# Block-sparse attention and gated feed-forward on one core: keys and sampled copies in one tile, scores in fewer and wider matmuls

## The chip, the cores and the metric

One NeuronCore of one Trainium2 chip. The metric is the device time in microseconds of one execution of the whole program. A core has five engines that run their own instruction queues: TensorE (PE in the profile; its weight loads are listed apart as PEld), VectorE (DVE), ScalarE (ACT), GpSimd (POOL) and SyncE (SP, which here only issues DMAs).

## The reference

The inputs are q, k, v of 4 batches, 8 heads, 768 positions and 64 channels, and, for each of the 24 blocks of 32 positions, three sampled block numbers. Attention is masked by blocks, and its output goes through a two-layer feed-forward network:

```python
scores = scale * np.matmul(q, k.transpose(0, 1, 3, 2))
mask = np.abs(blk_i - blk_j) <= 1
mask = mask | (blk_i == 0) | (blk_j == 0) | (blk_i == n_blocks - 1) | (blk_j == n_blocks - 1)
...
        mask[qb * block:(qb + 1) * block, kb * block:(kb + 1) * block] = True
scores = np.where(mask, scores, -1000000000.0)
attn = softmax(scores)
x = (attn @ v) as [3072, 512]
h = x @ w_in
sp = np.maximum(h, 0.0) + np.log1p(np.exp(-np.abs(h)))
out = (h * erf(sp)) @ w_out
```

So a middle block of 32 queries attends to 8 blocks of keys, 256 columns: its own and its two neighbours (96 columns), its three samples (96), and the first and the last block of the sequence (64). The first and the last block of queries attend to all 768 positions.

## The kernel before, in words

The work is cut into units of scores, sixteen per batch. A unit "m" holds four query blocks (j = 0 to 3) of one group t and two pairs of heads (r = 0, 1) of a half called quad; its scores are a PSUM tile `s_m` of 128 partitions by 1024 columns. There are ten m units a batch. Units "e" (two a batch) hold the two query blocks that are left over; units "f" (four a batch) hold the first and the last query block, against all keys. Keys and queries are float32; a head pair fills the 128 rows of the contraction, and `qm` holds the queries so that one block of 32 queries of two heads is a stationary operand of 128 rows by 64 columns.

The keys of a batch stand in `kx` (one of two buffers), ordered by block by `order_k` (line 120). The sampled blocks are copied by GpSimd from `kx` into small tiles `kg` (line 330, `gather`; four of them, one per query block, three copies each). `key_columns` (line 554) gives for one query block the three operands that `scores` (line 565) multiplies: 96 columns of neighbours from `kx`, 96 of samples from `kg`, 64 of the two end blocks from `kx`. For an m unit `scores` runs over r, then over the three parts, then over the four query blocks:

```python
for r in range(2):
    for part in range(3):
        for j in range(4):
            o = slice((j % 2) * 64, (j % 2) * 64 + 64)
            c, e, keys = key_columns(b, 1 + 4 * t + j, slice(0, P), pr)[part]
            pe.matmul(s4[o, j // 2, r, c:e], q_, keys, start=True, stop=True)
```

That is 24 matmuls. Odd and even j write to the upper and the lower 64 partitions, and so use the two halves of the array's columns. Each float32 matmul is two passes in the trace, each with a weight load of its own, so a unit has 48 MATMUL and 48 LDWEIGHTS records.

Behind the scores come a row maximum on VectorE, exponentials on ScalarE, a split into two float16 parts, a transposing DMA, and, two units later (`PV_LAG`), the product with gathered values `vb` (PE writes `po`; `values`, line 605). The feed-forward network is woven in: every step of the main loop (from line 978) issues on PE, in this order, 24 matmuls of the first layer (`h`), the values of an older unit if there are any (`po`), the scores of the next unit if it is its turn, and 12 matmuls of the second layer (`o`). The order on every engine is that in which the program issues. The first m units are issued by hand ahead of the loop, while weights are being loaded and decoded. `spare_k` (line 432) is the second key buffer, lent to the weight decoding until the second batch's keys arrive.

Of the kernel before, what the change touches and what calls it, by code (L numbers as in the profile page):

```python
# [9 lines left out]
F32 = mybir.dt.float32  # L10
I32 = mybir.dt.int32
# [7 lines left out]
P = 128  # L19
BLOCK = 32  # L20
# [22 lines left out]
def sparse_attention_moe(ctx: ExitStack, tc: tile.TileContext, qT, kT, v, sampled, w_in, w_out, out):  # L43
# [22 lines left out]
    pe, act, dve, pool, sp = (InOrder(e) for e in (nc.tensor, nc.scalar, nc.vector, nc.gpsimd, nc.sync))  # L66
    B, H, D, S = qT.shape
    NB = S // BLOCK
# [4 lines left out]
    NR = sampled.shape[1]  # L73
    KT = S // P
    HP = H // 2
    VW = 2 * D + 2
    NM = NB - 2
    MT = 5
    KGS, VGS = 4, 8
# [8 lines left out]
    cp = ctx.enter_context(tc.tile_pool(name="cp", bufs=1))  # L88
    ld = ctx.enter_context(tc.tile_pool(name="ld", bufs=2))
    at = ctx.enter_context(tc.tile_pool(name="at", bufs=2))  # L90
# [8 lines left out]
    act.preload_act_table_set("natural_log_exp_and_others")  # L99


    kxs = {}
    samp2 = at.tile([P, NB, NR, 2], I32, tag="xf", name="samp2", bufs=1)
    samp = cp.tile([P, NB * NR], I32, tag="samp", name="samp")

# [12 lines left out]
        krs[b, pr] = kr  # L118

    def order_k(b, pr):  # L120
        if b not in kxs:
            kxs[b] = ld.tile([P, NB + 1, HP, BLOCK], F32, tag="kx", name=f"kx_{b}", bufs=2)
        kr = krs.pop((b, pr))
        copy = pool.tensor_copy if b else dve.tensor_copy if pr > 1 else act.copy
        copy(kxs[b][:, :NB, pr, :], kr.rearrange("p (n c) -> p n c", c=BLOCK))
        copy(kxs[b][:, NB, pr, :], kr[:, :BLOCK])

# [1 line left out]
    qm = cp.tile([P, HP, 4, 2, BLOCK], F32, tag="qm", name="qm")  # L131
# [183 lines left out]
    kgs = {}  # L315
    POOL, SYNC = mybir.EngineType.Pool, mybir.EngineType.SP

    def block_numbers(first, last, engine):

        (load,), blocks = nc.values_load_multi_w_load_instructions(  # L320
            samp[0:1, first * NR : last * NR],
            [engine],
            min_val=0,
            max_val=NB,
            skip_runtime_bounds_check_because="sampled blocks are numbers of the sequence's blocks",
        )
        tc.keep_in_program_order(load)
        return blocks

    def gather(b, t):  # L330

        first, last = 1 + 4 * t, min(5 + 4 * t, NB - 1)
        blocks = block_numbers(first, last, POOL)
        for i in range(first, last):
            kg = at.tile([P, NR, HP * BLOCK], F32, tag="kg", name=f"kg_{b}_{i}", bufs=KGS)
            for r in range(NR):
                n = blocks[(i - first) * NR + r]
                pool.tensor_copy(
                    kg[:, r : r + 1],
                    kxs[b].rearrange("p n a c -> p n (a c)")[:, bass.ds(n, 1), :],  # L340
                )
            kgs[b, i] = kg.rearrange("p r (a c) -> p r a c", c=BLOCK)

    PLACES = ((3, 0), (0, 1), (1, 1))
    ring = iter(range(B * (NM + 3)))
# [83 lines left out]
    def slots(t, at_slot, n):  # L429
        return t[:, at_slot : at_slot + n, :].rearrange("p n c -> p (n c)").bitcast(I32)  # L430

    spare_k = ld.tile([P, NB + 1, HP, BLOCK], F32, tag="kx", name="spare_k", bufs=2)
    spare_k = spare_k.rearrange("p n a c -> p (n a c)").bitcast(I32)
    wide = spare_k[:, 2048:3072]

    def raw_of(key, i, n):
# [9 lines left out]
    apart = {}  # L446
# [104 lines left out]
        transpose(pT, p2)  # L551
        pts[unit] = pT

    def key_columns(b, i, rows, pr):

        kx, kg = kxs[b], kgs[b, i]
        return (
            (0, 96, kx[rows, i - 1 : i + 2, pr, :]),
            (96, 192, kg[rows, :, pr, :]),
            (192, 256, kx[rows, 0 : NB : NB - 1, pr, :]),  # L560
        )

    pts = {}

    def scores(unit):
        kind, b, n = unit[0], unit[1], unit[2:]
        tag = "_".join(str(x) for x in unit)
        s = ps_s.tile([P, 1024], F32, tag="s", name=f"s_{tag}")
        if kind == "m":

            t, quad = n
            s4 = s.rearrange("p (h r w) -> p h r w", h=2, r=2)
            for r in range(2):
                pr = 2 * quad + r
                for part in range(3):
                    for j in range(4):
                        o = slice((j % 2) * 64, (j % 2) * 64 + 64)
                        q_ = qm[:, pr, j].rearrange("p a c -> p (a c)")
                        c, e, keys = key_columns(b, 1 + 4 * t + j, slice(0, P), pr)[part]
                        pe.matmul(s4[o, j // 2, r, c:e], q_, keys, start=True, stop=True)  # L580
            softs[unit] = (s, 4, 256)
        elif kind == "e":
            (quad,) = n
            s3 = s.rearrange("p (r w) -> p r w", r=HP)
            for r in range(2):
                for part in range(3):
                    for j in range(2):
                        o = slice(j * 64, j * 64 + 64)
                        q_ = qm[:, 2 * quad + r, j].rearrange("p a c -> p (a c)")
                        c, e, keys = key_columns(b, NB - 3 + j, slice(0, P), 2 * quad + r)[part]  # L590
                        pe.matmul(s3[o, r, c:e], q_, keys, start=True, stop=True)
            softs[unit] = (s[:, :512], 2, 256)
        else:
            (pr,) = n
            q_ = qm[:, pr, 2:].rearrange("p n a c -> p (n a c)")
            for c, e in ((0, 512), (512, S)):
                keys = kxs[b][:, c // BLOCK : e // BLOCK, pr, :]
                pe.matmul(s[:, c:e], q_, keys, start=True, stop=True)
            softs[unit] = (s[:, :S], 1, S)

    xTs = {}
# [184 lines left out]
    def gathers(m):  # L786

        nonlocal kfree, vfree
        if kjobs and kfree >= 4 and kjobs[0][0] in have_k:
            kfree -= 4  # L790
            gather(*kjobs.pop(0))
        room = 4 if begun > 0 else VGS
        while vjobs and vjobs[0][0] in have_v:
            b, i = vjobs[0]
            n = 2 if i > 0 else 1
            fresh = b > 0 and 0 < i < VGS
            if vfree < n or room < n * (1 + fresh):
                break
            vfree -= n
            room -= n * (1 + fresh)  # L800
            vjobs.pop(0)
            gather_v(b, i) if i > 0 else whole_v(b, -1 - i)
# [12 lines left out]
    def behind(m):  # L815

        b, n = divmod(m, per)
        if b + 1 < B:
            c = b + 1
            if n == 10:  # L820
                load_q(c, 0)
            k = n if b else 2 * (n - 10) if n > 9 else -1
            if k in ((1, 3, 5, 7) if b else (2, 4, 6, 8)):
                order_k(c, (k - 1) // 2)
            if k in (0, 2, 4, 6):
                load_k(c, k // 2)
            if k == 8:
                have_k.add(c)
            if b == 0:
                n -= 4  # L830
            if n in (1, 7):
                load_v(c, 0)
            if n == 3:
                load_v(c, 1)
            if n in (2, 4):
                square_v(c, n // 2 - 1)
            if n == 5:
                scale_v(c)
            if n in (5, 6):
                split_v(c, 1, n - 5)  # L840
            if n in (8, 9):
                split_v(c, 0, n - 8)
            if n == 9:
                have_v.add(c)
# [46 lines left out]
    for pr in range(HP):  # L891
        order_k(0, pr)
# [9 lines left out]
    for quad in range(2):  # L902
        square_v(0, quad)
    scale_v(0)
    scores(units[0])
    split_v(0, 0, 0)
    split_v(0, 0, 1)
# [7 lines left out]
    have_v.add(0)  # L915

    scores(units[1])
    used_keys(units[1])
    gathers(0)
# [9 lines left out]

    soft_turn(units[1])  # L930
    scores(units[2])
    work("Di4 Qi4 Di5")
    soft_max(units[2])
# [44 lines left out]
    for m in range(len(groups) + FF_LAG):  # L978
        ch, i = divmod(m, NGR)
        steps = 0  # L980
        if ch < len(until):
            first = until[ch - 1] if ch else FIRST
# [91 lines left out]
```

## Time and profile before

| | |
|---|---|
| median of 3 runs | 841.46 us (836.75, 841.46, 845.61) |
| span of the profiled execution | 836.8 us |
| PE busy | 710.8 us, 85% |
| ACT / DVE / POOL busy | 601.1 / 554.4 / 123.7 us |
| records on PE | 11100 MATMUL, 11100 LDWEIGHTS |

The lowest of the three runs is the span to the rounding, so the profiled execution's own time is taken as 836.8 us, with nothing lying around it; the median of the runs is 4.7 us above it. Busy time is a sum over records that overlap each other in the pipeline; how long a stretch of work takes PE is read from the starts of its records in the timeline.

### The profile page before, as it was taken

The numbers are of one execution on the slowest core, as the hardware profiler recorded it, in microseconds if no ns is written. First come the engines' busy times: TensorE is split into PE (matmuls) and PEld (weight loads), VectorE is DVE, ScalarE is ACT, GpSimd is POOL, SyncE is SP. The second block draws the span as 40 slices with busy tenths as digits, with TensorE's granted clock in tenths as the row PEclk, the third lists the DMA queues.
The fourth block names the chain that finished last, engine by engine and source line by source line (L and its number), as shares of the span: only waits on it lengthen the run. The fifth ranks groups of instructions, "written<-read, shape, count | busy, mean of one in ns | idle before, by whom it ended". The sixth has DMA issues, their size and how long they took to land.

```text
span 836.8 us, 26712 instructions
## 1 busy us (share of the span) xinstructions
PE 710.8 (85%) x11100; PEld 504.8 (60%) x11100; DVE 554.4 (66%) x977; ACT 601.1 (72%) x999; POOL 123.7 (15%) x344
## 2 busy tenths in 40 slices
PE   1253637899897899899999899999999899999997
PEld 1252424566665667566777666667777576766664
DVE  3994796887764766766566676756677567654454
ACT  4654657987865766887768778868678678776774
POOL 5430111001222220100201231000111100000000
PEclk9775867989998999999999999999999999999999
DMA  8999953687899697661497886633576758211000
GB/s 325 297 257 318 243 120 90 164 207 164 172 212 209 178 205 198 186 131 45 136 216 178 210 198 192 167 79 83 117 167 166 190 103 188 53 33 40 1 27 26
DMA packets 199930, 131.61 MB, mean 157 GB/s; under 512 B 144000, under 2 KB 167168, under 8 KB 199808
## 3 DMA queue, kind: packets, MB, share of 16 engines
q1 hardware_dynamic: 196384, 118.10, 58.1%
q0 software_dynamic: 3424, 11.80, 4.3%
q8 instruction: 87, 1.43, 0.7%
q14 instruction: 35, 0.29, 0.1%
HBM read 83.88 MB, written 12.95 MB: 116 GB/s over the span
## 4 chain that ended last, share of the span: by engine, by line
PE 47%; DVE 15%; issue 12%; ACT 10%; DMA 10%; SPq 2%; POOL 2%; POOLq 1%; ACTq 0%
PE h L59 18%; PE o L59 18%; PE s_m L59 5%; DMA vb<-vtab 4%; PE po L59 3%; DVE g L59 2%; ACT pf_m L59 2%; DVE q L59 2%; DVE mx_m L59 2%; DMA vtab<-vn 2%; SPq L59 2%; ACT x L59 2%; DVE p_m L59 2%; POOL kg L59 2%; ACT q L59 2%
## 5 line engine op out<-in xcount | busy, mean ns | idle before, releaser
L59 PE MATMUL h<-xT,wi 128*128 128x256 f16 x2304 | 274.2, 276 | 14.9 <-ACT wi L59 7.5
L59 PE MATMUL o<-wo,g 128*128 128x512 f16 x1152 | 270.3, 385 | 7.9 <-DVE wo L59 4.0
L59 PEld LDWEIGHTS <-wi 128*128 128x128 f16 x2304 | 227.4, 99 | 65.5 <-ACT wi L59 8.8
L59 PEld LDWEIGHTS <-g 128*128 128x128 f16 x1152 | 110.3, 99 | 133.0 <-issue 14.8
L59 ACT ACTIVATE x<-x 128x512 f32<-128x512 f32 x288 | 181.5, 630 | 9.1
L59 POOL COPY kg<-kx 128x128 f32 x264 | 90.5, 394 | 286.2 <-PE s_m L59 183.6
L59 ACT ACTIVATE pf_m<-s_m,nb_m 128x256 f32<-128x256 f32 x160 | 62.7, 475 | 65.4 <-DVE nb_m L59 59.5
L59 DVE SCALAR_TENSOR_TENSOR q<-x,q 128x512 f32<-128x512 f32 x96 | 66.7, 695 | 61.4 <-ACT x L59 60.1
L59 ACT ACTIVATE x<-h,isg 128x512 f32<-128x512 f32 x96 | 65.2, 680 | 36.3 <-PE h L59 35.7
L59 PE MATMUL s_m<-kx,qm 128*64 128x64 f32 (+1 forms) x1280 | 75.0, 249 | 6.8 <-ACT pf_m L59 4.2
L59 ACT ACTIVATE q<-q 128x512 f32<-128x512 f32 x96 | 59.5, 620 | 29.6 <-DVE q L59 29.6
L59 DVE SCALAR_TENSOR_TENSOR q<-q,h 128x512 f32<-128x512 f32 x96 | 65.5, 682 | 22.6 <-ACT q L59 22.6
L59 DVE TENSOR_TENSOR p_m<-pf_m,p_m 128x1024 f16<-128x1024 f32 x40 | 49.3, 1232 | 32.3 <-ACT p_m L59 32.3
L59 DVE SCALAR_TENSOR_TENSOR g<-q,g 128x512 f16<-128x512 f32 x96 | 67.0, 698 | 3.3
L59 PE MATMUL po<-vb,pT_m 128*32 128x65 f16 (+1 forms) x3840 | 44.7, 201 | 25.7 <-DMA vb<-vtab 15.0
L59 PEld LDWEIGHTS s_m<-kx,qm 128*64 128x64 f32 x1280 | 59.7, 146 | 10.4 <-ACT pf_m L59 4.9
L59 ACT ACTIVATE q<-x 128x512 f32<-128x512 f32 x96 | 60.5, 630 | 3.1
L59 DVE TENSOR_REDUCE mx_m<-s_m 128x4 f32<-128x1024 f32 x40 | 48.8, 1219 | 20.2 <-PE s_m L59 20.2
L59 PEld LDWEIGHTS <-pT_m 128*32 128x32 f16 x3840 | 38.0, 97 | 36.8 <-DMA vb<-vtab 16.3
L59 PE MATMUL s_m<-kg,qm 128*64 128x96 f32 x640 | 46.9, 261 | 3.2 <-POOL kg L59 2.2
L59 DVE TENSOR_TENSOR x<-xf,x 128x512 f16<-128x512 f32 x24 | 16.9, 703 | 43.3 <-ACT x L59 43.3
L59 DVE TENSOR_SCALAR g<-q 128x512 f16<-128x512 f32 x96 | 41.3, 431 | 3.3
(115 smaller groups left out, 623.7 us busy)
## 6 DMA issues: line engine op xcount, KB each, us to landing
vb<-vtab SPq DMA_DIRECT2D x280, 65.0 KB, 2.9
vb<-vtab SPq DMA_DIRECT2D x32, 390.0 KB, 4.1
vraw<-in_v_dram SPq DMA_DIRECT2D x10, 768.0 KB, 5.1
vtab<-vn SPq DMA_DIRECT2D x16, 390.0 KB, 5.4
vb<-vtab SPq DMA_DIRECT2D x12, 520.0 KB, 5.0
qt<-in_qT_dram SPq DMA_DIRECT2D x20, 256.0 KB, 3.3
out_dram<-wo SPq DMA_DIRECT2D x20, 256.0 KB, 4.3
vb<-vtab SPq DMA_DIRECT2D x36, 130.0 KB, 3.0
```

Source lines behind the costliest of these rows:

```text
L59: done = call(*args, **kwargs)
```

## The change

All keys and sampled copies live in one tile `keys` of 62 slots of one block each: 25 slots for even batches, 25 for odd ones, and a ring of 4 x 3 slots for the sampled copies. One access pattern can then step from a block's three neighbours to its three samples, so these are one moving operand of 192 columns (`near_keys`). The end keys are the same for every query block, so two query blocks (128 stationary columns) are multiplied with them at once (`end_keys`). An m unit now has 4 matmuls of 128 stationary columns by 64 moving ones, then 8 of 64 by 192; an e unit does one of the first kind and two of the second, twice. `order_k` and `gather` write to the new places; `spare_k` is the odd batches' part of `keys`. f units multiply the same operands as before.

```diff
+    NKEY = 2 * (NB + 1)
+    keys = cp.tile([P, NKEY + KGS * NR, HP * BLOCK], F32, tag="keys", name="keys")
+    kring = iter(range(B * NM))
+    def key_blocks(b):
+        return keys[:, b % 2 * (NB + 1) : (b % 2 + 1) * (NB + 1)]
...
-            kg = at.tile([P, NR, HP * BLOCK], F32, tag="kg", name=f"kg_{b}_{i}", bufs=KGS)
+            kgs[b, i] = k = NKEY + next(kring) % KGS * NR
             for r in range(NR):
                 n = blocks[(i - first) * NR + r]
-                pool.tensor_copy(
-                    kg[:, r : r + 1],
-                    kxs[b].rearrange("p n a c -> p n (a c)")[:, bass.ds(n, 1), :],
-                )
+                pool.tensor_copy(keys[:, k + r : k + r + 1], key_blocks(b)[:, bass.ds(n, 1), :])
...
+    def near_keys(b, i, pr):
+        c = slice(pr * BLOCK, (pr + 1) * BLOCK)
+        first = b % 2 * (NB + 1) + i - 1
+        near = keys[:, first : first + NR, c]
+        apart = (kgs[b, i] - first) * HP * BLOCK
+        return bass.AP(near.tensor, near.offset, [near.ap[0], (apart, 2), near.ap[1], near.ap[2]])
+    def end_keys(b, pr):
+        return key_blocks(b)[:, 0 : NB : NB - 1, pr * BLOCK : (pr + 1) * BLOCK]
...
             for r in range(2):
                 pr = 2 * quad + r
-                for part in range(3):
-                    for j in range(4):
-                        o = slice((j % 2) * 64, (j % 2) * 64 + 64)
-                        q_ = qm[:, pr, j].rearrange("p a c -> p (a c)")
-                        c, e, keys = key_columns(b, 1 + 4 * t + j, slice(0, P), pr)[part]
-                        pe.matmul(s4[o, j // 2, r, c:e], q_, keys, start=True, stop=True)
+                for g in range(2):
+                    q_ = qm[:, pr, 2 * g : 2 * g + 2].rearrange("p j a c -> p (j a c)")
+                    pe.matmul(s4[:, g, r, 192:], q_, end_keys(b, pr), start=True, stop=True)
+            for r in range(2):
+                pr = 2 * quad + r
+                for j in range(4):
+                    o = slice((j % 2) * 64, (j % 2) * 64 + 64)
+                    q_ = qm[:, pr, j].rearrange("p a c -> p (a c)")
+                    pe.matmul(s4[o, j // 2, r, :192], q_, near_keys(b, 1 + 4 * t + j, pr), start=True, stop=True)
             softs[unit] = (s, 4, 256)
         elif kind == "e":
...
             for r in range(2):
-                for part in range(3):
-                    for j in range(2):
...
+                pr = 2 * quad + r
+                q_ = qm[:, pr, :2].rearrange("p j a c -> p (j a c)")
+                pe.matmul(s3[:, r, 192:], q_, end_keys(b, pr), start=True, stop=True)
+                for j in range(2):
...
+                    pe.matmul(s3[o, r, :192], q_, near_keys(b, NB - 3 + j, pr), start=True, stop=True)
```

On TensorE, at the third m unit of the third batch (unit `s_m_2_1_0`), there stand before, for the first of its two head pairs, behind the last product with values, four matmuls with neighbours, four with samples and four with end keys (sizes are output partitions by moving columns); the six rows from the neighbours on then come again for the second pair:

```order
L59 MATMUL po_2_0_0_7466<-vb_89,pT_m_2_0_0_7069 32x65
L59 MATMUL s_m_2_1_0_7638<-kx_2_3810,qm_87 64x96 x4
L59 MATMUL s_m_2_1_0_7638<-kg_2_5_7588,qm_87 64x96
L59 MATMUL s_m_2_1_0_7638<-kg_2_6_7592,qm_87 64x96
L59 MATMUL s_m_2_1_0_7638<-kg_2_7_7596,qm_87 64x96
L59 MATMUL s_m_2_1_0_7638<-kg_2_8_7600,qm_87 64x96
L59 MATMUL s_m_2_1_0_7638<-kx_2_3810,qm_87 64x64 x4
```

At the same place the changed program has, for both head pairs together:

```order
L59 LDWEIGHTS pT_m_2_0_0_6742
L59 MATMUL po_2_0_0_7126<-vb_90,pT_m_2_0_0_6742 32x65
L59 MATMUL s_m_2_1_0_7294<-keys_85,qm_88 128x64 x4
L59 MATMUL s_m_2_1_0_7294<-keys_85,qm_88 64x192 x8
L59 LDWEIGHTS g_1_1_2_7047
L59 MATMUL o_1_1_0_0_6783<-wo_104,g_1_1_2_7047 128x512
```

The end keys have moved ahead of everything else in the unit, as four matmuls of full width; eight matmuls of half width follow, and then the second layer as before.

On TensorE, at the first e unit of the third batch (`s_e_2_0`), there stand before, for the first head pair (the second repeats them):

```order
L59 MATMUL po_2_4_1_9893<-vb_89,pT_m_2_4_1_9654 32x65
L59 MATMUL s_e_2_0_9991<-kx_2_3810,qm_87 64x96 x2
L59 MATMUL s_e_2_0_9991<-kg_2_21_9805,qm_87 64x96
L59 MATMUL s_e_2_0_9991<-kg_2_22_9809,qm_87 64x96
L59 MATMUL s_e_2_0_9991<-kx_2_3810,qm_87 64x64 x2
```

The changed program has there, for both head pairs:

```order
L59 MATMUL po_2_4_1_9439<-vb_90,pT_m_2_4_1_9202 32x65
L59 MATMUL s_e_2_0_9537<-keys_85,qm_88 128x64
L59 MATMUL s_e_2_0_9537<-keys_85,qm_88 64x192 x2
L59 MATMUL s_e_2_0_9537<-keys_85,qm_88 128x64
L59 MATMUL s_e_2_0_9537<-keys_85,qm_88 64x192 x2
L59 LDWEIGHTS g_2_0_0_9363
```

Here full and half width alternate: the end keys of the second pair stand between two runs of half width. On VectorE, ScalarE, GpSimd and SyncE the same instructions stand in the same order as before.

## Rows read from the trace of the kernel before

**Rows 1.** The page, its head: span, and busy time, share and records of engines.

```profile
span 836.8 us, 26712 instructions
...
PE 710.8 (85%) x11100; PEld 504.8 (60%) x11100; DVE 554.4 (66%) x977; ACT 601.1 (72%) x999; POOL 123.7 (15%) x344
```

**Rows 2.** Busy time (us) of each engine in three stretches, granted clock, DMA share.

```profile
core 0: us, PE busy (x) PEld busy (x) DVE busy (x) ACT busy (x) POOL busy (x), PEclk, DMA share, GB/s
0.00:60.00 60.00, 20.67 (x338) 18.40 (x338) 45.83 (x72) 34.43 (x60) 26.49 (x63) 0.83 0.94 295
60.00:138.00 78.00, 38.17 (x747) 26.88 (x748) 53.27 (x83) 44.18 (x69) 11.87 (x30) 0.69 0.71 195
138.00:836.80 698.80, 651.92 (x10039) 459.54 (x10025) 455.30 (x824) 522.44 (x870) 85.37 (x252) 0.98 0.60 141
```

**Rows 3.** The chain that ended last, its shares by line from 380 to 430 us.

```profile
by line: PE h L59 40.4%; PE o L59 36.9%; PE s_m L59 12.2%; PE po L59 6.3%; PE s_f L59 2.6%; issue 1.9%
```

**Rows 4.** Timeline of PE, one m unit: start, length, operation, records.

```profile
417.73 0.55 PE L59 MATMUL s_m<-kx,qm 128*64 128x96 f32 x8
418.11 0.50 PE L59 MATMUL s_m<-kg,qm 128*64 128x96 f32 x8
418.44 0.73 PE L59 MATMUL s_m<-kx,qm 128*64 128x64 f32 x16
419.00 0.50 PE L59 MATMUL s_m<-kg,qm 128*64 128x96 f32 x8
419.33 0.40 PE L59 MATMUL s_m<-kx,qm 128*64 128x64 f32 x8
419.67 0.61 PE L59 MATMUL o<-wo,g 128*128 128x512 f16 x2
```

**Rows 5.** Timeline of PEld, windows of 516.70:516.80 and 516.81:516.90: weight loads of 128 columns.

```profile
516.72 0.19 PEld L59 LDWEIGHTS s_f<-kx,qm 128*128 128x128 f32 x1 [0.88 <-ACT pf_m L59]
...
516.72 0.30 PEld L59 LDWEIGHTS s_f<-kx,qm 128*128 128x128 f32 x2 [0.88 <-ACT pf_m L59]
```

**Rows 6.** Timeline of PE, two windows near 61.3 us: passes of one column.

```profile
61.30 0.27 PE L59 MATMUL whole_wi<-one,top_wi 128*128 128x1 f32 x1 [1.36 <-DVE top_wi L59]
...
61.30 0.38 PE L59 MATMUL whole_wi<-one,top_wi 128*128 128x1 f32 x2 [1.36 <-DVE top_wi L59]
```

**Rows 7.** Timeline of PE, 384.5:396.5: an f unit and an m unit, each behind h.

```profile
384.40 2.78 PE L59 MATMUL h<-xT,wi 128*128 128x256 f16 x24
387.02 1.46 PE L59 MATMUL s_f<-kx,qm 128*128 128x512 f32 x4
388.32 2.75 PE L59 MATMUL o<-wo,g 128*128 128x512 f16 x12
390.91 2.78 PE L59 MATMUL h<-xT,wi 128*128 128x256 f16 x24
393.62 0.55 PE L59 MATMUL s_m<-kx,qm 128*64 128x96 f32 x8
```

**Rows 8.** Timeline of PE, 514.5:518.5: an f unit behind a wait.

```profile
516.72 1.56 PE L59 MATMUL s_f<-kx,qm 128*128 128x512 f32 x4 [0.77 <-ACT pf_m L59]
518.12 0.59 PE L59 MATMUL o<-wo,g 128*128 128x512 f16 x2
```

**Rows 9.** Timeline of PE, 375.5:377: an e unit.

```profile
375.55 0.39 PE L59 MATMUL s_e<-kx,qm 128*64 128x96 f32 x4
...
376.59 0.60 PE L59 MATMUL o<-wo,g 128*128 128x512 f16 x2
```

**Rows 10.** PE's groups from 138 us on: records, busy us, mean ns, idle before.

```profile
L59 PE MATMUL s_m<-kg,qm 128*64 128x96 f32 x528 | 37.6, 252 | 3.2 <-POOL kg L59 2.2 <-POOL vn L59 1.0
L59 PE MATMUL po<-vb,pT_m 128*32 128x65 f16 x2205 | 37.0, 200 | 14.0 <-DMA pT_m<-p_m 7.8 <-DMA vb<-vtab 5.7
...
L59 PE MATMUL s_m<-kx,qm 128*64 128x64 f32 x528 | 29.4, 225 | 1.0 <-issue 1.0
...
L59 PE MATMUL s_e<-kg,qm 128*64 128x96 f32 x64 | 5.8, 247 | 2.0 <-issue 2.0
```

**Rows 11.** Tile kg: what its writers and readers waited for (us, times).

```profile
  PE s_m L59: 183.6, 10
```

More of the change, by code (lines that the diff above doesn't have):

```diff
@@ L99, in sparse_attention_moe @@
     act.preload_act_table_set("natural_log_exp_and_others")
-    kxs = {}
+    NKEY = 2 * (NB + 1)
[3 more added lines that the diff above has]
+        return keys[:, b % 2 * (NB + 1) : (b % 2 + 1) * (NB + 1)]
     samp2 = at.tile([P, NB, NR, 2], I32, tag="xf", name="samp2", bufs=1)
@@ L120, in order_k @@
     def order_k(b, pr):
-        if b not in kxs:
-            kxs[b] = ld.tile([P, NB + 1, HP, BLOCK], F32, tag="kx", name=f"kx_{b}", bufs=2)
+        kx = key_blocks(b).rearrange("p n (a c) -> p n a c", c=BLOCK)
         kr = krs.pop((b, pr))
         copy = pool.tensor_copy if b else dve.tensor_copy if pr > 1 else act.copy
-        copy(kxs[b][:, :NB, pr, :], kr.rearrange("p (n c) -> p n c", c=BLOCK))
-        copy(kxs[b][:, NB, pr, :], kr[:, :BLOCK])
+        copy(kx[:, :NB, pr, :], kr.rearrange("p (n c) -> p n c", c=BLOCK))
+        copy(kx[:, NB, pr, :], kr[:, :BLOCK])
     qts = {}
@@ L334, in gather @@
         for i in range(first, last):
-            kg = at.tile([P, NR, HP * BLOCK], F32, tag="kg", name=f"kg_{b}_{i}", bufs=KGS)
+            kgs[b, i] = k = NKEY + next(kring) % KGS * NR
             for r in range(NR):
                 n = blocks[(i - first) * NR + r]
-                pool.tensor_copy(
-                    kg[:, r : r + 1],
-                    kxs[b].rearrange("p n a c -> p n (a c)")[:, bass.ds(n, 1), :],
-                )
-            kgs[b, i] = kg.rearrange("p r (a c) -> p r a c", c=BLOCK)
+                pool.tensor_copy(keys[:, k + r : k + r + 1], key_blocks(b)[:, bass.ds(n, 1), :])
     PLACES = ((3, 0), (0, 1), (1, 1))
@@ L430, in slots @@
         return t[:, at_slot : at_slot + n, :].rearrange("p n c -> p (n c)").bitcast(I32)
-    spare_k = ld.tile([P, NB + 1, HP, BLOCK], F32, tag="kx", name="spare_k", bufs=2)
-    spare_k = spare_k.rearrange("p n a c -> p (n a c)").bitcast(I32)
+    spare_k = key_blocks(1).rearrange("p n c -> p (n c)").bitcast(I32)
     wide = spare_k[:, 2048:3072]
@@ L552, in soft_turn @@
         pts[unit] = pT
[L554 to L561, printed above, removed]
+    def near_keys(b, i, pr):
[6 more added lines that the diff above has]
+        return key_blocks(b)[:, 0 : NB : NB - 1, pr * BLOCK : (pr + 1) * BLOCK]
     pts = {}
@@ L585, in scores @@
             for r in range(2):
-                for part in range(3):
-                    for j in range(2):
[L588 to L591, printed above, removed]
+                pr = 2 * quad + r
+                q_ = qm[:, pr, :2].rearrange("p j a c -> p (j a c)")
+                pe.matmul(s3[:, r, 192:], q_, end_keys(b, pr), start=True, stop=True)
+                for j in range(2):
+                    o = slice(j * 64, j * 64 + 64)
+                    q_ = qm[:, pr, j].rearrange("p a c -> p (a c)")
+                    pe.matmul(s3[o, r, :192], q_, near_keys(b, NB - 3 + j, pr), start=True, stop=True)
             softs[unit] = (s[:, :512], 2, 256)
@@ L596, in scores @@
             for c, e in ((0, 512), (512, S)):
-                keys = kxs[b][:, c // BLOCK : e // BLOCK, pr, :]
-                pe.matmul(s[:, c:e], q_, keys, start=True, stop=True)
+                k = key_blocks(b)[:, c // BLOCK : e // BLOCK, pr * BLOCK : (pr + 1) * BLOCK]
+                pe.matmul(s[:, c:e], q_, k, start=True, stop=True)
             softs[unit] = (s[:, :S], 1, S)
```

## The prediction

> **What bounds the kernel now.** I read the page's head first [rows 1]: PE is busy for 710.8 of 836.8 us, more than any other engine. A mean over the span hides the stages, so the busy time by stretch came next [rows 2]. Up to 138 us nothing is near its limit: PE has 20.67 of 60 us, then 38.17 of 78, at a granted clock of 0.83 and 0.69, while weights and values are loaded and decoded. From 138 us on PE is busy for 651.92 of 698.80 us at a granted clock of 0.98, of which 1.00 is the 2.4 GHz level; ACT has 522.44, DVE 455.30. The chain in a quiet stretch of that stage is PE from end to end, 12.2% of it scores of m units and 1.9% issue [rows 3]. So there a nanosecond of PE is nearly a nanosecond of the result, and the question is how long PE takes over one unit of scores, before and after.
>
> **One m unit before** [rows 4]. From its first record to the first of the second layer: 419.67 - 417.73 = 1.94 us. The pieces follow from the starts, since the lengths overlap. The eight records with samples start at 418.11 and their successor at 418.44: 0.33 us. Odd and even query blocks run side by side in the two halves of the array, so these are four pairs, 0.0825 us each for 96 columns. Between 418.44 and 419.00 stand eight records with end keys and eight with neighbours, 0.56 us; less 0.33 that leaves 0.23 us, 0.058 a pair of 64 columns. The first group takes 0.38, so 0.05 us is a weight load that nothing covers. From the last group, 419.33 + 0.23 = 419.56, to `o` it is another 0.11 us.
>
> **What the parts of the change cost.** Four things go into the new unit.
>
> A wide float32 pass streams 0.85 ns a column: the f unit behind `h` goes from 387.02 to 388.32, 1.30 us for 2 x 512 + 2 x 256 columns [rows 7]. The side-by-side pairs have the same rate (0.0825 / 96 = 0.86). So 192 columns take 0.163 us a pair, and merging neighbours and samples saves next to nothing in streaming: 8 x 0.163 = 1.30 us in place of 16 x 0.0825 = 1.32. The loads that go were hidden already, except where streams are short.
>
> A wide float32 load takes twice as long as a half-wide one, and the streams beside it are as short as before. One load of 128 columns lasts 0.19 us, two in succession 0.30 [rows 5], so the second ends 0.11 us behind the first. Two passes of a single column, each with such a load, show the same: 0.27 us for one, 0.38 for both [rows 6]. The pass with end keys streams 64 columns, 0.054 us, and so can't hide a load of 0.11. The pairs before took 0.058 with two half-wide loads. Bounds for one wide pass are therefore 0.058 (all hidden) and 0.11; I take 0.11, since both rows that have wide loads in succession show it.
>
> A change of the array's width has a price. From `h` to the f unit, both full width, it is 387.02 - 384.40 = 2.62 us for 24 records; from `h` to the m unit, 393.62 - 390.91 = 2.71 [rows 7]. The step to half width costs 0.09 us, and the load behind it lies open, 0.05 more [rows 4]. Behind a wait a wide load lies open with 0.10: the f unit takes 518.12 - 516.72 = 1.40 us [rows 8] where it takes 1.30 behind `h`. The old unit changed width when it began and when it ended; the new one changes once more, between end keys and the rest.
>
> Four pairs of 96 columns with their loads take 0.33 us [rows 4], which is the streaming rate alone, so narrow loads hide behind streams of other records. A rule speaks against that: the Trainium skill, "TensorE: Matmul & The Clock Gate", section "The mechanism" of its part on packing small matmuls, says that a weight load overlaps a running matmul only when the row groups differ. Here all loads use all rows, so none would overlap. By it the unit before would be 24 loads longer than its streams, and the trace disagrees; what it would make of the change is the third rival.
>
> The new m unit, from the same start: open load 0.10, seven more passes at 0.11 = 0.77, the last stream 0.05; width change and open load 0.14; eight pairs 1.30; end to `o` 0.11. Together 2.47 to 2.48 us against 1.94: **+0.54 us**. For the three m units that begin a batch and stand behind `h`, the old unit pays 0.09 for its step to half width (2.03), and the new one starts at full width with its load hidden (2.38): +0.35. An e unit takes 376.59 - 375.55 = 1.04 us [rows 9]. The new one: 0.10 + 0.11 + 0.05 + 0.14 + 2 x 0.163 = 0.73 for the first head pair; for the second the same with 0.09 for going back to full width, 0.82; 0.11 to `o`: 1.66, **+0.62 us**.
>
> The 528 records with samples from 138 us on are 33 m units of 16, three of them behind `h`; 64 records in e units are 8 units of 8 [rows 10]. The sum on PE is 30 x 0.54 + 3 x 0.35 + 8 x 0.62 = 16.2 + 1.05 + 5.0 = **+22.2 us**.
>
> What else moves. The first seven m units lie ahead of 138 us, where PE idles for most of the time; half of 7 x 0.54 is +2 (bounds 0 and 7.6, all of it at half clock). PE waits that longer scores would fill: from 138 us on it idles for 698.80 - 651.92 = 46.9 us, of which 14.0 us are waits of `po` for transposing and gathering DMAs [rows 10]. Most waits hang on scores that are late too; where a unit of scores lies between a wait and its cause, the wait shrinks by that unit's growth. About eight such waits give -4 (bounds 0 and -10). Fewer instructions mean fewer stalls of issue: an m unit had 96 records and has 48. The groups of scores show 3.0 us of issue idle together in the rows at hand [rows 10], of which I take -0.5 (bounds 0 and -3). GpSimd may start a copy into the ring a little later, because the half-width matmuls that release the slots now come last in the unit; it waited 183.6 us for such matmuls [rows 11], while PE waited 2.2 us for the copies in the whole stage [rows 10], so I cost it at nothing; what hides it is that GpSimd is busy for only 85.37 of 698.80 us [rows 2], and without that cover it would be some 0.2 us (two or three pairs) in each of 20 groups of four blocks, 4 us. The new place of the keys, the changed dependences and the lent buffer I also cost at nothing: every other engine has its old order, and the copies wait for the same matmuls' successors.
>
> Against the profiled execution: 836.8 + 22.2 + 2 - 4 - 0.5 = 856.5 us. The median of the runs shown lies 4.7 us above that execution, and a median is what is asked for: 841.5 + 19.7 = **861 us**.
>
> **The rivals.**
>
> Only the change of width costs; wide loads are hidden after all, at 0.058 a pass. The new m unit is then 7 x 0.052 = 0.36 us shorter, +0.17; a unit behind `h` +0.0; an e unit +0.52. 30 x 0.17 + 8 x 0.52 = 9.3, with the small terms +7.5: 849 us. For it: the old pairs load 128 columns, in two halves, in 0.058. Against: the two wide loads that end 0.11 apart [rows 5, 6].
>
> Neither costs: a full-width load takes 0.058 because both halves load side by side, and the array goes from full to half width between units of one float32 stream without the 0.09. Then 16 x 0.0825 + 8 x 0.058 = 1.78 becomes 8 x 0.163 + 8 x 0.058 = 1.77, and with fewer instructions -1: 840 us, not slower. It decides from the point at which the end keys of a unit take no more than 0.47 us. Against it stand two kinds of rows [rows 5, 7].
>
> No load overlaps a stream (the rule above). Then 24 pairs of loads at 0.05 before (1.20 us) become 8 wide at 0.11 and 8 pairs at 0.05 (1.28), and the change of width adds 0.09: +0.15 a unit, +0.3 an e unit, 30 x 0.15 + 8 x 0.3 = 7, less some 2 filled waits: 847 us. The 0.33 us of rows 4 speaks against it.
>
> PE is held by instruction supply more than its idle time tells, and half the records of scores free it: issue is 1.9% of the chain in a quiet stretch [rows 3], 13 us if that held for all 698.8. If two thirds of it went, 9 us, and nothing were lost elsewhere, it would be 832 us. It needs hidden loads and the free change of width too.
>
> Worse than forecast: the moving operand that jumps from neighbours to samples in far-off slots streams slower than 0.85 ns a column. At half as much again, 8 x 0.08 = 0.65 us a unit, 33 units and 8 e units at 0.33 add some 24 us: 885. Nothing in the rows shows it; operands with gaps every 32 columns stream at the full rate already.
>
> **How the numbers follow.** Forecast 0.69; width alone 0.12; neither 0.10; no overlap 0.02; issue 0.03; jump 0.04. The forecast's own range, with the bounds of its small terms and 0.5% of scatter between runs, is 852 to 871. The whole range of 847 to 870 takes in most of that and the greater part of the rival at 849, and leaves the cases at 840 and below and at 885 outside. A measurement of this kernel can tell about 1% from no change, so slower starts at 849.9 and faster ends at 833.0. Slower: 0.69 + 0.04 + 0.04 of the width rival (it straddles the line) = 0.77. Same: 0.08 + 0.10 + 0.02 + 0.01 = 0.21. Faster: 0.02.
>
> **What would show it.** In the changed profile an m unit's timeline should have eight full-width records that start 0.11 us apart, a gap of about 0.14, then pairs 0.163 apart, and 2.45 to 2.5 us from its first record to `o`; an e unit 1.6 to 1.7. PE's busy time from 138 us on should rise by about 20 us, with the other engines' unchanged. Full-width records 0.06 apart would make the width rival right, no gap as well the one after it; the forecast is wrong if a unit takes under 2.2 us, or if it takes 2.5 and the span doesn't follow.

## The result, and the profile after

The changed kernel takes 844.34 us (median of 22 runs, 838.37 to 848.77), the kernel before 839.84 us in 22 runs beside it: a ratio of 1.0053, 95% interval 1.0037 to 1.0070. That is a small loss, within the 1% that the forecast counted as no change, and below the forecast range of 847 to 870. The profiled spans are 836.8 and 843.5 us, +6.7; what follows accounts for these two executions, while the medians lie 4.5 us apart. Ratios here and below leave out one execution of the kernel before that took 1243.62 us at a granted clock of 0.57.

The page's head after, and its line on fetched instructions (queue, packets, MB, share):

```profile
span 843.5 us, 24600 instructions
...
PE 742.9 (88%) x10044; PEld 513.2 (61%) x10044; DVE 554.4 (66%) x977; ACT 601.3 (71%) x999; POOL 125.9 (15%) x344
...
q8 instruction: 79, 1.29, 0.6%
```

PE is busy 32 us longer than in [rows 1]; the other engines are where they were. The third stretch, columns as in [rows 2]:

```profile
138.00:843.50 705.50, 677.47 (x9215) 465.90 (x9212) 457.16 (x826) 522.77 (x871) 86.80 (x252) 0.98 0.59 140
```

Against [rows 2], PE is busy for 25.55 us more in a stretch that is only 6.70 us longer. (Busy time counts records that overlap once, and is not a sum over them: 528 records with a mean of 252 ns are 37.6 us in [rows 10].) Its idle time fell from 46.88 to 28.03 us, by 18.85. So the new work is there, and most of it stands where PE stood idle before.

The timeline of PE after, an m unit and its next work, then an e unit and its next work:

```profile
449.67 2.56 PE L59 MATMUL s_m<-keys,qm 128*128 128x64 f32 x24
452.16 0.39 PE L59 MATMUL o<-wo,g 128*128 128x512 f16 x1
...
557.80 1.75 PE L59 MATMUL s_e<-keys,qm 128*128 128x64 f32 x12
559.49 0.60 PE L59 MATMUL o<-wo,g 128*128 128x512 f16 x2
```

From start to start the m unit takes 452.16 - 449.67 = 2.49 us (forecast 2.47 to 2.48; [rows 4] give 1.94) and the e unit 1.69 (forecast 1.66). The first pass alone, then two passes, of the same m unit:

```profile
449.67 0.32 PE L59 MATMUL s_m<-keys,qm 128*128 128x64 f32 x1
...
449.67 0.43 PE L59 MATMUL s_m<-keys,qm 128*128 128x64 f32 x2
```

0.43 - 0.32 = 0.11 us: the full-width passes with end keys run at the pace of their loads, as [rows 5, 6] said. The half-width pairs behind them start 0.1625 us apart.

PE's groups from 138 us on, columns as in [rows 10]:

```profile
L59 PE MATMUL o<-wo,g 128*128 128x512 f16 x1140 | 265.0, 383 | 1.0 <-DVE g L59 0.8
...
L59 PE MATMUL s_m<-keys,qm 128*64 128x192 f32 x528 | 55.5, 349 | 0.8 <-POOL keys L59 0.8
L59 PE MATMUL s_m<-keys,qm 128*128 128x64 f32 x264 | 37.6, 288 | 0.0
L59 PE MATMUL po<-vb,pT_m 128*32 128x65 f16 x2240 | 35.8, 198 | 8.4 <-DMA vb<-vtab 3.4 <-DMA pT_m<-p_m 3.1 <-DVE mx_f L59 1.6
```

`po` waits 8.4 us where it waited 14.0 [rows 10]; `o` waits 1.0 us, before it was 4.9, of which 3.2 for VectorE's `wo`. Summed over all groups, PE's waits of 0.05 us and more went from 35.4 to 19.2 us for other engines and DMAs (-16.2), and from 7.0 to 4.3 us for issue (-2.6).

**Where the added time was taken up.** The same steps of the main loop can be laid side by side by the start of their first-layer matmuls. The lag of the changed kernel grows by about half a microsecond with each unit of scores and drops at a few waits. Step 42 starts at 457.56 us before and 463.59 after (+6.03), step 43 at 466.99 and 469.69 (+2.70). Between them the timeline of before has

```profile
462.90 4.26 PE L59 MATMUL o<-wo,g 128*128 128x512 f16 x12 [2.56 <-DVE wo L59]
466.99 1.25 PE L59 MATMUL h<-xT,wi 128*128 128x256 f16 x10
```

and that of after

```profile
466.20 2.75 PE L59 MATMUL o<-wo,g 128*128 128x512 f16 x12
469.69 1.58 PE L59 MATMUL h<-xT,wi 128*128 128x256 f16 x13 [0.73 <-DVE m_v L59]
```

The wait of before is for VectorE, which scales a piece of `wo`. Timeline of VectorE before and, behind the dots, after:

```profile
462.10 0.75 DVE L59 TENSOR_SCALAR wo<-o,iso 128x512 f32<-128x512 f32 x1
...
465.17 0.75 DVE L59 TENSOR_SCALAR wo<-o,iso 128x512 f32<-128x512 f32 x1
```

VectorE, too, is later after, but by 3.07 us where PE is 6.03 later. PE found the work done, and the wait of 2.56 us was gone. Two more places: waits of before,

```profile
255.74 0.21 PE L59 MATMUL po<-vb,pT_m 128*32 128x65 f16 x2 [0.61 <-DMA pT_m<-p_m]
260.97 0.21 PE L59 MATMUL po<-vb,pT_m 128*32 128x65 f16 x1 [5.02 <-DMA vb<-vtab]
...
657.04 1.47 PE L59 MATMUL po<-vb,pT_m 128*32 128x65 f16 x96 [3.54 <-DMA pT_m<-p_m]
```

and the same matmuls after:

```profile
260.15 0.19 PE L59 MATMUL po<-vb,pT_m 128*32 128x65 f16 x1 [0.35 <-DMA vb<-vtab]
261.13 0.21 PE L59 MATMUL po<-vb,pT_m 128*32 128x65 f16 x4 [0.79 <-DMA vb<-vtab]
262.11 1.04 PE L59 MATMUL po<-vb,pT_m 128*32 128x65 f16 x89 [0.76 <-DMA vb<-vtab]
...
661.83 0.96 PE L59 MATMUL po<-vb,pT_m 128*32 128x65 f16 x96
```

There the lag went from +4.53 to +1.32 us and from +8.40 to +3.84 us.

The same comparison can be made for every wait of before: the instruction or DMA that ended it has its counterpart in the changed trace. Waits over 0.15 us for other engines and DMAs make 34.8 us from 138 us on. For 20.0 us of them what ended the wait had fallen behind by at least 1 us less than PE had (at 261 us the gathered values even landed 0.8 us earlier, while PE was 4.5 late); for 10.1 us it had kept within 0.5 us of PE's lag or fallen further behind; 4.7 us lie between.

**Where some was added.** Three times it jumped: from -0.43 to +3.92 at 248 us, behind a wait of 1.54 us for gathered values at 239 us; from -0.72 to +4.17 at 383 us; and from +3.29 to +6.54 at 600 us. The third place, timeline of after:

```profile
593.02 0.37 PE L59 MATMUL po<-vb,pT_f 128*32 128x64 f16 x13 [1.54 <-issue]
593.33 3.81 PE L59 MATMUL s_m<-keys,qm 128*128 128x64 f32 x24
597.07 3.13 PE L59 MATMUL o<-wo,g 128*128 128x512 f16 x12
```

PE waited 1.54 us for issue, and then the unit took 3.74 us in place of 2.49 and the second layer 2.97 in place of 2.60. The busy time by stretch shows why, after, one line for each of the three:

```profile
239.50:246.30 6.80, 6.80 (x89) 4.67 (x74) 3.25 (x9) 0.82 (x2) 1.97 (x6) 0.50 0.97 254
376.00:382.80 6.80, 6.80 (x22) 2.94 (x23) 3.66 (x9) 1.99 (x4) 1.94 (x6) 0.50 0.01 2
594.40:597.80 3.40, 3.40 (x19) 1.89 (x19) 0.59 (x1) 0.00 (x0) 1.17 (x5) 0.51 0.59 165
```

The granted clock was 0.50 to 0.51, the 1.2 GHz level. Before and after have five such stretches each from 138 us up to the last matmul. Eight of the ten lie in or just behind one long wait of PE, such as those of 2.56 and 3.54 us above, and two behind a row of shorter ones (three for gathered values, shown above; four for GpSimd's copies). What the lower level cost is estimated as half of PE's busy time in these stretches: 9.1 us before, 13.1 after, +4.0.

So from 138 us on the sum closes: +21.5 us of work (25.55 - 4.0), +4.0 by the lower clock, -16.2 of waits for others, -2.6 of issue: +6.7. But the cut at 138 us is the same time and not the same place of the program: the changed kernel is already late there, by 2.4 us at the fifth step of the loop (142.84 and 145.27 us), and work of that size was moved behind the cut. From the fifth step on the span grows by 4.3 us: +19.1 of work, and the other three terms as they are.

### The profile page after: what moved, and what is told of

It is laid out like the page before. It is cut to its first block, busy times and chain, and to the rows that moved or that the text cites. A ratio compares the mean times of both kernels' runs of the same rounds, so it can differ in the third digit from the quotient of the medians.

```text
span 843.5 us, 24600 instructions
## 1 busy us (share of the span) xinstructions
PE 742.9 (88%) x10044; PEld 513.2 (61%) x10044; DVE 554.4 (66%) x977; ACT 601.3 (71%) x999; POOL 125.9 (15%) x344
## 3 DMA queue, kind: packets, MB, share of 16 engines
q8 instruction: 79, 1.29, 0.6%
## 4 chain that ended last, share of the span: by engine, by line
PE 47%; DVE 19%; DMA 13%; ACT 12%; issue 5%; SPq 3%; POOL 0%; ACTq 0%; POOLq 0%
PE h L59 18%; PE o L59 17%; PE s_m L59 6%; DMA vb<-vtab 5%; PE po L59 3%; DVE g L59 3%; DVE q L59 3%; DMA vtab<-vn 3%; SPq L59 3%; DVE mx_m L59 3%; ACT x L59 3%; DMA vraw<-in_v_dram 3%; ACT pf_m L59 2%; ACT q L59 2%; DVE p_m L59 2%
## 5 line engine op out<-in xcount | busy, mean ns | idle before, releaser
L59 PEld LDWEIGHTS <-g 128*128 128x128 f16 x1152 | 110.5, 99 | 138.2 <-issue 22.1
L59 POOL COPY keys<-keys 128x128 f32 x264 | 92.9, 404 | 296.6 <-PE s_m L59 190.1
L59 PE MATMUL s_m<-keys,qm 128*64 128x192 f32 (+1 forms) x960 | 117.1, 344 | 4.5 <-ACT pf_m L59 3.7
L59 PEld LDWEIGHTS s_m<-keys,qm 128*64 128x64 f32 (+1 forms) x960 | 90.9, 171 | 18.4 <-ACT pf_m L59 4.7
L59 ACT ACTIVATE p_m<-pf_m 128x1024 f16<-128x1024 f32 x40 | 42.3, 1057 | 1.3
```

What stands on the lines that cost most here:

```text
L59: done = call(*args, **kwargs)
```

## The experiments

The texts on record speak of four theories. **A**: PE's longer units are taken up by waits for chains that don't hang on PE's pace, so a first half microsecond a unit costs little and a second costs more. **B**: fewer instructions give back some 15 us of supply, whatever the waits do. **S** came after the first four runs: what counts is not the number of PE's instructions but where the dense runs of short matmuls fall in the blocks in which instructions arrive. **N**: that position doesn't matter. All ratios are against the kernel before in the same job. Matmuls that are added write where the real scores are written afterwards.

**Longer units, otherwise the kernel before.** One matmul (two for the second kernel) ahead of the scores of each m and e unit:

```diff
+            for _ in range(1):
+                pe.matmul(s[:64, :320], qm[:, 0, 0].rearrange("p a c -> p (a c)"), kxs[b][:, :10, 0, :], start=True, stop=True)
```

> The kernel before, with one more half-width float32 matmul of 320 columns (0.54 us of PE, overwritten by the unit itself) ahead of every m and e unit; nothing else differs. Theory A, PE is not the only bound: extra PE time is swallowed where PE waits for chains of the other engines and of the DMA queues, so 0.54 us a unit costs as little as it did in the change: ratio 1.003 to 1.010, PE's idle time from 138 us on falls by 12 us or more. Theory B, the 22 us were paid in full and the halved number of records gave some 15 back through instruction supply: ratio 1.020 to 1.030 here, since records rise.

> As the run with one extra matmul, with two of them: 1.09 us a unit. Theory A: the waits that swallowed the first half are nearly used up, so the second half costs more than the first: ratio 1.015 to 1.028, and the increase over one extra matmul is over twice what the first cost. Theory B: linear, 1.045 to 1.055.

An m unit with one extra matmul, timeline of PE, its first records and its next work:

```profile
451.10 1.00 PE L59 MATMUL s_m<-kx,qm 128*64 128x320 f32 x9
...
453.57 2.76 PE L59 MATMUL o<-wo,g 128*128 128x512 f16 x12
```

Measured: an m unit of 453.57 - 451.10 = 2.47 us gave 849.32 us, 1.0096 [1.0067, 1.0126]; one of 3.01 us, with two extra matmuls, gave 862.68 us, 1.0258 [1.0213, 1.0302]; before 842.06. The first 0.53 us a unit (22 us in 41 units, about what the change adds) cost 7.3 us, the next 0.54 us (22 us) cost 13.4. PE's waits other than issue from 138 us on shrank from 35.4 to 21.8 and 15.3 us. Both ratios lie in A's ranges, the first at the upper end, and far from B's. Two things that A had said were missed: the second step cost 1.8 times the first and not over twice, and with one matmul PE's idle time fell by 9.7 us and not 12 or more (46.9 to 37.2), since issue waits grew by 4.0 (7.0 to 11.0).

**Each half of the change alone.** First the changed kernel with the end keys per query block again, then the kernel before with the end keys at full width and neighbours and samples apart:

```diff
-                for g in range(2):
-                    q_ = qm[:, pr, 2 * g : 2 * g + 2].rearrange("p j a c -> p (j a c)")
-                    pe.matmul(s4[:, g, r, 192:], q_, end_keys(b, pr), start=True, stop=True)
+                for j in range(4):
+                    o = slice((j % 2) * 64, (j % 2) * 64 + 64)
+                    q_ = qm[:, pr, j].rearrange("p a c -> p (a c)")
+                    pe.matmul(s4[o, j // 2, r, 192:], q_, end_keys(b, pr), start=True, stop=True)
```

```diff
-                for part in range(3):
+                for g in range(2):
+                    q_ = qm[:, pr, 2 * g : 2 * g + 2].rearrange("p j a c -> p (j a c)")
+                    pe.matmul(s4[:, g, r, 192:], q_, kxs[b][:, 0 : NB : NB - 1, pr, :], start=True, stop=True)
+            for r in range(2):
+                pr = 2 * quad + r
+                for part in range(2):
```

> The changed kernel with the end keys multiplied per query block at half width as before; neighbours and samples stay one operand of 192 columns. A unit has 32 MATMUL records (before 48, change 24) and should take 1.92 us of PE, 0.02 less than before. Theory A: no difference from before, ratio 0.996 to 1.002. Theory B: two thirds of what the fewer records give without the cost, 10 us: ratio 0.985 to 0.991.

> The kernel before with the end keys multiplied for two blocks at once at full width, ahead of the rest, and neighbours and samples apart as before: 40 MATMUL records a unit and the whole cost of the change on PE (2.49 us). Theory A: like the change, ratio 1.003 to 1.009. Theory B: only a third of the relief, ratio 1.015 to 1.022.

Measured: 842.55 us, 0.9999 [0.9969, 1.0030], with a unit of 1.92 us; and 856.35 us, 1.0182 [1.0152, 1.0211], with one of 2.51 us. The first takes a third of the scores' records away and gains nothing, against B. The second missed A's range and fell in B's, though its unit is hardly longer than that of the first padded kernel, which had more records and took 7 us less. A number of records can't explain that pair. What stood out was PE's issue time from 138 us on: 13.1 us, against 11.0 in the first padded kernel, 8.8 with the merged operand and 4.3 after. Its amount alone explains little (over the whole span the merged operand has 13.9 us as well, and lost nothing), but the places led further. Waits for issue of the kernel with wide end keys, whole span:

```profile
PE po L59 <- issue: 11.6, 7, 2.7
PE s_e L59 <- issue: 1.7, 1, 1.7
PE o L59 <- issue: 0.5, 1, 0.5
```

(total us, times, longest). Number all records of PE's queue from 0 in order of start: loads, matmuls and the 98 to 101 semaphore and drain records that stand between them. These waits then stand at records whose number leaves 193 or 194 when divided by 256. In the profiles of all fourteen kernels every issue wait over 0.3 us does, 91 of 91. The page's instruction queue carries 79 packets of 1.29 MB in all after (87 and 1.43 before), 16 KB each. The Trainium skill says in "Runtime: NRT & Kernel Launch", section "Instruction fetch mechanics", that an engine's instructions come in 16 KiB blocks of 256, which agrees with the 16 KB packets and the 256. It calls the crossing mostly hidden, and by number it is: 1172 blocks of the fourteen profiles end at such a place, and 91 ends have a wait over 0.3 us. But a block that PE uses up in under 2.3 us, as in the dense runs of `po` and scores, is followed by such a wait, 0.5 to 2.7 us long, in 57 of 69 cases; one that lasts over 3.2 us in 18 of 1031. That is a count of what the traces show; why the wait falls at 193 and not at 0 they don't say.

**Moving the blocks.** 64 tiny matmuls at the very start, when PE is idle, shift all later instructions by 128, half a block:

```diff
     pool.memset(one, 1.0)
+    lead = ps_h.tile([P, 512], F32, tag="h", name="lead")
+    one16 = one.bitcast(F16)
+    for _ in range(64):
+        pe.matmul(lead[:32, :1], one16[:, 1:2].to_broadcast([P, 32]), one16[:, 1:2], start=True, stop=True)
```

> The kernel with the wide end keys alone, with 64 tiny matmuls (128 PE instructions, nothing reads them) at the very start, where PE idles; all later PE instructions move by 128 places in the instruction stream, half of a 16 KB block of 256. Theory S: what sets the kernels of the first set apart beyond PE time is stalls of PE's instruction supply, which depend on where block ends fall against dense runs of short matmuls; this kernel showed 13.1 us of them, the most, so moved by half a block it should lose several: ratio 1.004 to 1.013 (it was 1.018), issue idle 4 to 9 us. Theory N: the stalls are chance of one profile, and the time stays: 1.015 to 1.021.

> The changed kernel with the same 128 instructions ahead. It showed 4.3 us of issue idle after 138 us, the least of all. Theory S: moved by half a block it has more, 7 to 13 us, and the time goes up: ratio 1.008 to 1.018 (it was 1.005). Theory N: unchanged, 1.002 to 1.008.

> The kernel before with the same 128 instructions ahead (7.0 us of issue idle without them). Theory S: the issue idle changes by some us either way and the time follows it: ratio between 0.993 and 1.007, with the sign of the change of issue idle. Theory N: 0.998 to 1.002 whatever the profile shows.

> The kernel with merged neighbours and samples and half-width end keys, with the same 128 instructions ahead (8.8 us of issue idle without them, ratio 0.9999). Theory S: issue idle between 3 and 9 us, the time follows it: 0.990 to 1.001. Theory N: 0.997 to 1.003.

Measured (before 843.14 us in this job):

| kernel with the shift | median us | ratio [95%] | issue, whole span: unshifted, shifted |
|---|---|---|---|
| end keys at full width only | 847.88 | 1.0073 [1.0046, 1.0100] | 13.9, 4.5 |
| after | 847.80 | 1.0072 [1.0043, 1.0101] | 4.6, 7.2 |
| before | 845.63 | 1.0045 [1.0014, 1.0076] | 8.1, 13.4 |
| merged operand only | 840.12 | 0.9980 [0.9953, 1.0007] | 13.9, 10.3 |

From 138 us on, where the expectations count it, issue went from 13.1 to 3.5, from 4.3 to 6.4, from 7.0 to 9.8 and from 8.8 to 8.8 us, in the order of the rows. The kernel with wide end keys went from 1.0182 to 1.0073 (in two jobs, each against its own runs of before) by a shift that adds no work where PE is busy: N falls for it, by over 1%. The rest is weaker. The kernel before lost 0.45%, in S's range and outside N's; but in its profile it is 6.1 us late at the first step of the loop already, behind a wait for issue of 3.58 us at 84.6 us, and 8.3 at the end. The changed kernel lies in N's range and below S's, in its ratio (1.0072 against 1.0053, intervals that overlap) and with 6.4 us of issue where S had 7 to 13. The merged operand fits both. The largest piece in the kernel with wide end keys is at the second e unit of the second batch. Unshifted, timeline of PE:

```profile
379.42 0.19 PE L59 MATMUL po<-vb,pT_f 128*32 128x65 f16 x1 [2.27 <-issue]
379.54 1.01 PE L59 MATMUL s_e<-kx,qm 128*128 128x64 f32 x6
...
382.26 4.89 PE L59 MATMUL o<-wo,g 128*128 128x512 f16 x12
386.99 0.27 PE L59 MATMUL h<-xT,wi 128*128 128x256 f16 x1
```

Shifted, the same unit:

```profile
376.38 0.62 PE L59 MATMUL po<-vb,pT_f 128*32 128x65 f16 x30
376.92 0.75 PE L59 MATMUL s_e<-kx,qm 128*128 128x64 f32 x6
...
378.62 2.76 PE L59 MATMUL o<-wo,g 128*128 128x512 f16 x12
381.22 2.78 PE L59 MATMUL h<-xT,wi 128*128 128x256 f16 x24
```

Behind the wait of 2.27 us the granted clock was down (0.63 from 379 to 382 us, 1.00 in the shifted kernel), and so the e unit took 2.72 us in place of 1.70 and the second layer 4.73 in place of 2.60: one stall of 2.27 us cost 5.4, of the 8.5 us between the two spans. By the starts of the steps the unshifted kernel is 0.2 us behind the shifted one ahead of this place, 5.8 behind it, and 8.5 at the end. Not every stall costs something: another at 206.4 us, of 2.67, has no lower clock behind it, and in the shifted kernel its place is taken by

```profile
205.88 0.75 PE L59 MATMUL s_e<-kx,qm 128*128 128x64 f32 x6 [2.75 <-ACT pf_f L59]
```

**Where in the program the work is added.** Two small extra matmuls in every m and e unit of the kernel before (base), made sixteen times as wide in four units only: in the first four m units of the second batch, or in the last two m and both e units of the last batch. The number of instructions is the same in all three; the widening adds 4 x 1.485 = 5.9 us (an m unit takes 3.65 us in place of 2.165).

```diff
+            wide = 16 if b == 1 and n[0] < 2 else 1
+            for _ in range(2):
+                pe.matmul(s[:64, : wide * 32], qm[:, 0, 0].rearrange("p a c -> p (a c)"), kxs[b][:, :wide, 0, :], start=True, stop=True)
```

> The kernel before with two extra half-width matmuls of 32 columns ahead of every m and e unit (some 0.25 us of PE each unit, results overwritten). It is the common base for the two runs beside it, which have the same number of PE instructions in the same places, so that the ends of the 256-instruction blocks fall alike. Alone: ratio 1.000 to 1.012.

> As the base, but in the first four m units of the second batch the two extra matmuls have 512 columns: 6 us more of PE time, all of it ahead of the place (some 261 us) where PE waits for gathered values and, a little later, for copies of sampled keys. Theory A (extra PE time vanishes where a chain of other engines or queues ends last): 0 to 2.5 us over the base. Rival (PE is the bound throughout, linear): 5.5 to 6.5 us.

> As the base, but the long extra matmuls stand in the last two m units and both e units of the last batch: the same 6 us of PE time, behind the last long wait of PE for another chain. Theory A and the linear rival alike: 5 to 6.5 us over the base; theory A is wrong if this is as cheap as the early place.

Measured: base 848.14 us, 1.0051 [1.0015, 1.0087]; early 849.18, 1.0087 [1.0052, 1.0121]; late 854.87, 1.0152 [1.0096, 1.0207]; before 842.52. The early 5.9 us cost 1.0 us by the medians (3.0 by the ratios), the late 6.7 (8.5). The direction is A's, the size less sure: the intervals overlap a little, early is inside the expected 0 to 2.5 us by the medians and over it by the ratios, and late is over its 5 to 6.5 by both. (In the late profile the last e unit took 4.44 us where the base took 2.17, both at the lower clock: 0.8 us more than the widening.) The timelines show part of the early work being taken up, 1.5 us of it at this wait. Base:

```profile
261.80 0.21 PE L59 MATMUL po<-vb,pT_m 128*32 128x65 f16 x1 [3.69 <-DMA vb<-vtab]
```

Early:

```profile
263.81 0.19 PE L59 MATMUL po<-vb,pT_m 128*32 128x65 f16 x1 [2.15 <-DMA vb<-vtab]
```

**A placement chosen by count.** The merged operand alone, with 55 tiny matmuls ahead in place of 64, a number picked so that few blocks fall into dense runs:

> Merged neighbours and samples, half-width end keys, and 110 instead of 128 tiny PE instructions ahead. All stalls of PE's instruction supply in the ten profiles so far stand at record 193 or 194 of 256; counted on the recorded starts, 110 is the lead with which the fewest blocks of 256 are used up in under 3.2 us (8, against 9 to 10 with 0 or 128, and 13 in the kernel before). Theory S: issue idle under 7 us, ratio 0.990 to 0.998. Theory N: 0.997 to 1.003.

Measured: 839.77 us, 0.9965 [0.9932, 0.9998], issue 8.3 us, of which 6.9 from 138 us on. The ratio is S's, but N's range begins at 0.997, within the interval, so this doesn't part the two. It is the fastest version here, 0.35% ahead of the kernel before with an interval that ends just short of 1, and 0.9% ahead of the change by the ratios. As a gain over before it is marginal.

## Why the prediction was wrong

**What held.** The working on PE did, term by term: the full-width pass at 0.11 us, 2.49 us for an m unit and 1.69 for an e unit. With the measured units the sum of +22.2 us is 30 x 0.55 + 3 x 0.35 + 8 x 0.64 = 22.7. PE's busy time without the clock's share agrees less well: +21.5 us from 138 us on, 2.4 of them work that the prologue's lag moved behind that cut; from the fifth step on +19.1, where the units behind it would give 22.1. These 3 us stay open. The prologue's +2 is +2.4. GpSimd's copies, costed at nothing, cost nothing: the m units waited 0.8 us for them, before 2.2. The rivals with hidden loads or a free change of width are out with the 0.11, the jumping operand with the 0.1625. The rivals at 847, 840 and 849 come closest in time (2.7, 4.3 and 4.7 us off), for reasons that the units' times refute. Of its two signs of being wrong the forecast met the second: a unit takes 2.5 us and the span doesn't follow.

**The step that failed** is "About eight such waits give -4 (bounds 0 and -10)", with its ground "Most waits hang on scores that are late too". Waits for other engines and DMAs fell by 16.2 us, beyond that bound. Most of them didn't keep pace with PE: PE waited for decoded weights from VectorE and ScalarE, gathered values, transposing DMAs and GpSimd's copies, and for 20.0 of 34.8 us what ended the wait fell behind by at least 1 us less than PE did. When PE comes later, such a chain is further on or done, and what PE lost in the steps before, it gets back there. What holds each of these chains instead was not followed up. I had read "a nanosecond of PE is nearly a nanosecond of the result" off a busy share of 93% and a chain in a quiet stretch [rows 2, 3]; the 35 us of waits lie in other stretches, and a chain through one of them would have shown an engine that bounds it instead. The two padded kernels show it without the change: 22 us more on PE cost 7.3, the next 22 cost 13.4.

**A term that was missing.** The forecast has no clock in it. Some stalls and other waits are followed by work at the lower level, so where the waits lie decides a few microseconds either way: +4.0 in this profile, by the estimate above.

**Issue.** I took -0.5 with bounds of 0 and -3; it was -2.6. Right in its bounds, but by accident: I tied it to the number of records, and the runs tie it to where blocks of 256 end. Laying the changed program, with as many records, half a block later gave 7.2 us of issue in place of 4.6 over the whole span.

**The base.** An execution's time lies some 1.75 us above its span (853.44 and 851.7 for one kernel here), while I set them equal and so put the median 4.7 us above this execution. With 839.84 for before in the later runs, that term is about 1.7 us too high.

**Sums that don't come out.** The forecast's own range of 852 to 871 is narrower at its lower end than the bounds of its terms: 861 - 2 - 6 - 2.5 = 850.5, ahead of any scatter. In the rival at 849 the terms as listed add up to 9.3 + 2 - 4 - 0.5 = +6.8, not +7.5. Neither changes the outcome.

Put in order: 22.2 and 2 together became 21.5 (19.1 from the fifth step on and the prologue's 2.4); -4 became -16.2; -0.5 became -2.6; 0 for the clock became +4.0.

## What to carry to other kernels

Doubling the width of a stationary operand whose stream is short makes its load the pace: here 0.11 us a pass in place of 0.058, and the wider matmul was slower per unit though it halved the records of the end keys. An engine that is busy for 93% of a stage may still be waiting in it for chains of their own pace; list its waits, ask of each whether its cause would move with the engine, and count the others as slack ahead of any price for added (or saved) work. Before a difference of 1% is put down to an edit, look where PE's issue waits lie: shift the program by some idle-time instructions and measure again.

## What was not expected of the hardware

All 91 issue waits over 0.3 us sit at one place in blocks of 256 records of PE's queue, and a shift of 128 records changed one kernel's time by 1.1% (1.0182 to 1.0073). A stall of 2.27 us cost 5.4, because the granted clock fell behind it and PE's next matmuls ran at the lower level. That is not the rule: of 120 waits of PE over 1.5 us from 138 us on, in all fourteen profiles, 61 have no stretch at the lower level close behind them (within 7 us). Not settled: what part of the change's remaining +0.5% would go with a better placement (its own, with 4.6 us of issue, has the second lowest issue time of the fourteen profiles); whether its fewer records are worth anything, since the first padded kernel, with as much work added and more records, is 0.4% slower by ratios whose intervals touch (1.0096 [1.0067, 1.0126] and 1.0053 [1.0037, 1.0070]); and why merging neighbours and samples into one operand shows no gain beyond scatter.
